# Three score banks in batch 0, fillers accumulating in the value bank, and the small sum instructions on one engine

## The chip, the cores and the metric

One NeuronCore of one Trainium2 chip runs the whole program. TensorE (PE in the profile) multiplies and writes to PSUM, a small memory of eight banks. ScalarE (ACT), VectorE (DVE) and GpSimd (POOL) do the element-wise work, the first two also out of PSUM; SyncE (SP) issues the loads and stores. The metric is the device time of one execution in microseconds; a profile shows one such execution.

## What is computed

The reference is an attention over a window of 128 keys, a gated block with a convolution over three positions, and a second gated block with a causal convolution over five positions. Shapes: 4 batches, 8 heads of 64, 576 positions, model width 512, inner width 1024.

```python
scores = scale * np.matmul(q, k.transpose(0, 1, 3, 2))
scores = np.where(mask, scores + bias[None], -1000000000.0)
attn = np.exp(scores - np.max(scores, axis=-1, keepdims=True))
attn = attn / (np.sum(attn, axis=-1, keepdims=True) + 1e-09)
x = np.matmul(attn, v)                      # heads joined to width 512

h = np.maximum(x @ w_in, 0.0)               # first block
conv = sum(conv_w[k] * shifted(h, k - 1) for k in range(3))
x = (h * sigmoid(conv)) @ w_out

pre = sum(conv_w2[k] * shifted(x, k - 4) for k in range(5))
out = (sigmoid(pre) * (x @ w_val)) @ w_out2 # second block
```

The weights come in double precision, and the kernel works to about single precision: each operand of a large product is split into a high and a low part, and three products (high by high, high by low, low by high) are added in PSUM.

## The kernel before

The work is cut into eight units: four batches (`b`), each in two parts of the sequence (`u` = 0: positions 0 to 255, `u` = 1: the rest). Attention for one unit runs over four pairs of heads; the dense part of a unit runs `hidden` (x by `w_in`, relu, convolution, gate), `mixed` (by `w_out`, second convolution), `valued` (by `w_val`) and `output` (by `w_out2`) in this order. While one unit's dense part runs, the next unit's attention is worked in between.

**Attention of one pair** (`attention`, lines 490 to 682). Blocks of 64 queries of both heads are taken two at a time as a group; a group's scores lie in one PSUM bank of the ring `ps_s` (tiles `pss`). L546 multiplies q by k, L550 adds the bias `bm` and finds the row minimum of the negated scores, L558 takes the exponential and its row sum on ScalarE, L561 (on VectorE) or L563 (on GpSimd) adds 1e-9 to the group's sums and scales them (an instruction on 128x2 numbers), and the reciprocal L568 on VectorE follows. In batch 0 (`turn`) the exponentials are transposed on TensorE: L576 (VectorE) or L577 (GpSimd) makes a unit matrix scaled by the reciprocals (`dg`), L584 multiplies by it into the same `pss` bank, and L590 (ScalarE) and L592 (VectorE) read the high and the low part out to `pt`. In the other batches L609 and L611 scale in place and a DMA transposes. L651 multiplies by V into the one bank `psx`, and L667, or L672 and L674, read that bank out as x.

**V's scale** (`vmax`, `vscale`). V is loaded (tile `gts` for the first half of batch 0, `raw` else), L444 takes its maximum on VectorE, L459 and two small matmuls (L464 and L478, which also write to `psx`) bring it to every partition, and L482 or L483 reads it out.

**Weights** (`widen`, lines 374 to 411). A piece of 128x512 weights arrives as double precision in a `raw` buffer (three of them, 512 KB each) and is turned into single precision by two instructions on ScalarE (L390, L392) and two on VectorE (L394, L403), then split by a copy (L409 on ScalarE or L410 on GpSimd) and a subtraction on GpSimd (L368). There are 24 such pieces, 8 of `w_in`, 8 of `w_out`, 4 of `w_val` and 4 of `w_out2`, and they are all worked while batch 0 runs.

**What sets the order.** `Program` (lines 39 to 209) plans all instructions in lists with costs of its own: each step has an engine, or a choice of engines (L565 gives such a choice), a cost, a priority and the keys it reads and writes. The plan gives each engine's queue its order, and every engine works its queue strictly in that order. A ring of buffers hands them out in the order of the program; `spare = (20,)` on `ps_s` (L321) holds the last of the three banks back for the first 20 groups, which are those of batch 0, so that these use two banks.

**Fillers.** Where the plan shows TensorE idle for more than 250 ns, `warm` (lines 855 to 860) puts matmuls on the zero tile `idle` into TensorE's queue. They go to the third `pss` bank, which nobody else uses until batch 1, and they stop at the first score that needs it (`first`, L862).

## Time and profile before

| | us |
|---|---|
| median of three runs | 455.79 |
| lowest and highest of the three | 453.82, 456.14 |
| the profiled execution's own time | 454.31 |
| its span, first to last instruction | 452.5 |
| busy in the span: TensorE | 436.9 |
| VectorE | 342.7 |
| ScalarE | 319.9 |
| GpSimd | 201.9 |

The 1.8 us between the profiled execution's time and its span lie around the instructions. TensorE's busy time contains the fillers (193 of them, 25.9 us by the profile's count, in which neighbours overlap), so it is no measure of useful work in the early part. The profile's views that follow are the busy times by stretch, the instructions in order of time for one engine, the list of waits, and the list for one source line.

### The profile page before, as it was taken

What the parts mean: (1) busy time and instruction counts of PE and PEld (TensorE: products, weight loads), DVE (VectorE), ACT (ScalarE), POOL (GpSimd) and SP (SyncE); (2) the same over time, 40 slices, a digit from 0 to 9 for tenths busy, and PEclk for the clock granted to TensorE, in tenths of its full rate; (3) what the DMA queues carried; (4) which work ended last, traced back from release to release, by engine and by line L of the source; (5) the groups of instructions that cost most, each with busy time, mean ns of one, the idle gap of its engine ahead of it and who ended that gap; (6) DMA issues with size and microseconds to landing.
All of it is one profiled execution on the core that took longest, in us unless ns stands there. A gap on an engine that the chain in (4) does not pass through costs nothing.

```text
span 452.5 us, 10277 instructions
## 1 busy us (share of the span) xinstructions
PE 436.9 (97%) x3605; PEld 412.1 (91%) x3605; DVE 342.7 (76%) x1056; ACT 319.9 (71%) x930; POOL 201.9 (45%) x341
## 2 busy tenths in 40 slices
PE   7988999999999999999999999999999999999997
PEld 5667888899999999999999999998999998998996
DVE  5799988998977558995969479967979487917390
ACT  2799999964867668785974578677956576847442
POOL 1477898881553327030560436041722164454511
PEclk9999999999999999999999999999999999999999
DMA  8665757557264525658441527395352429350001
GB/s 268 221 233 198 236 171 236 178 183 250 81 100 99 129 67 114 163 128 173 132 81 49 110 77 134 103 189 138 63 112 67 128 64 170 90 119 1 0 1 59
DMA packets 75235, 57.85 MB, mean 128 GB/s; under 512 B 55984, under 2 KB 65968, under 8 KB 75184
## 3 DMA queue, kind: packets, MB, share of 16 engines
q1 hardware_dynamic: 75184, 57.21, 48.6%
q8 instruction: 28, 0.46, 0.4%
q14 instruction: 23, 0.19, 0.1%
HBM read 39.10 MB, written 4.72 MB: 97 GB/s over the span
## 4 chain that ended last, share of the span: by engine, by line
PE 59%; DVE 15%; ACT 13%; DMA 7%; issue 4%; POOL 1%; SPq 0%; DVEq 0%; ACTq 0%; POOLq 0%
PE pm L691 17%; PE pm L692 15%; PE pm L693 15%; PE pss L546 5%; DVE gts L353 4%; PE psx L651 4%; DMA pt<-p 3%; DVE t L353 2%; ACT sg L390 2%; DMA raw<-in_w_in 2%; DVE pss L550 1%; ACT pss L558 1%; PE pss L584 1%; ACT pm L392 1%; DMA raw<-in_w_val 1%
## 5 line engine op out<-in xcount | busy, mean ns | idle before, releaser
L691 PE MATMUL pm<-x,win 128*128 128x256 f32 (+1 forms) x256 | 80.9, 316 | 2.1 <-DVE t L353 2.0
L691 PE MATMUL pm<-g,wout 128*128 128x254 f32 (+1 forms) x256 | 79.8, 312 | 0.2
L692 PE MATMUL pm<-g,wout 128*128 128x254 f32 (+1 forms) x256 | 76.1, 297 | 0.0
L692 PE MATMUL pm<-x,win 128*128 128x256 f32 (+1 forms) x256 | 76.0, 297 | 0.0
L693 PE MATMUL pm<-x,win 128*128 128x256 f32 (+1 forms) x256 | 75.8, 296 | 0.0
L693 PE MATMUL pm<-g,wout 128*128 128x254 f32 (+1 forms) x256 | 75.7, 296 | 0.0
L353 DVE SCALAR_TENSOR_TENSOR t<-pm,cc,t 128x325 f32<-128x325 f32 (+3 forms) x112 | 56.1, 513 | 15.1 <-ACT t L346 11.9
L368 POOL TENSOR_TENSOR g<-t,g 128x254 fp32r<-128x254 f32 (+1 forms) x64 | 51.9, 814 | 28.2 <-ACT g L337 25.5
L546 PE MATMUL pss<-qk 128*128 128x192 f32 (+2 forms) x288 | 57.5, 322 | 3.9 <-DVE pt L592 3.0
L550 DVE CUSTOM_DVE_ANT_0 pss<-pss,bm 128x192 f32<-128x192 f32 (+2 forms) x144 | 47.9, 339 | 14.9 <-PE pss L546 12.9
L563 POOL TENSOR_SCALAR st<-st 128x2 f32<-128x2 f32 (+1 forms) x56 | 11.1, 199 | 103.6 <-ACT pss L558 87.8
L353 DVE SCALAR_TENSOR_TENSOR gts<-pm,cc,gts 128x322 f32<-128x322 f32 (+4 forms) x120 | 57.2, 506 | 0.1
L558 ACT ACTIVATE pss<-pss,st 128x192 f32<-128x192 f32 (+2 forms) x108 | 40.7, 377 | 17.2 <-DVE st L550 15.8
L691 PEld LDWEIGHTS pm<-x,win 128*128 128x128 f32 x256 | 48.2, 188 | 5.0 <-DVE t L353 3.4
L546 PEld LDWEIGHTS pss<-qk 128*128 128x128 f32 x288 | 44.3, 192 | 7.4 <-DVE pt L592 5.7
L691 PEld LDWEIGHTS pm<-g,wout 128*128 128x128 f32 x256 | 48.2, 188 | 1.6 <-ACT pm L392 0.3
L692 PEld LDWEIGHTS pm<-g,wout 128*128 128x128 f32 x256 | 48.5, 190 | 0.0
L693 PEld LDWEIGHTS pm<-g,wout 128*128 128x128 f32 x256 | 48.5, 190 | 0.0
L692 PEld LDWEIGHTS pm<-x,win 128*128 128x128 f32 x256 | 48.3, 189 | 0.0
L693 PEld LDWEIGHTS pm<-x,win 128*128 128x128 f32 x256 | 48.2, 188 | 0.0
L611 DVE SCALAR_TENSOR_TENSOR p<-pss,st,p 128x192 f16<-128x192 f32 (+1 forms) x103 | 36.4, 386 | 12.8 <-DMA pt<-p 9.0
L609 ACT ACTIVATE p<-pss,st 128x192 f16<-128x192 f32 (+1 forms) x103 | 35.9, 403 | 14.0 <-DMA pt<-p 10.2
(109 smaller groups left out, 1172.4 us busy)
## 6 DMA issues: line engine op xcount, KB each, us to landing
qk<-in_qk SPq DMA_DIRECT2D x16, 544.0 KB, 3.7
qk<-in_qk SPq DMA_DIRECT2D x16, 384.0 KB, 3.5
raw<-in_w_out SPq DMA_DIRECT2D x12, 512.0 KB, 4.0
vr<-in_vN SPq DMA_DIRECT2D x16, 256.0 KB, 3.0
raw<-in_w_in SPq DMA_DIRECT2D x8, 512.0 KB, 3.9
raw<-in_vN SPq DMA_DIRECT2D x8, 384.0 KB, 4.4
out<-t SPq DMA_DIRECT2D x16, 161.0 KB, 1.9
raw<-in_w_val SPq DMA_DIRECT2D x4, 512.0 KB, 3.5
```

The source lines that it names most:

```text
L353: pg.add("DVE", dve_t(n, 0 if isinstance(scalar, float) else 1), lambda: nc.vector.scalar_tensor_tensor(out=out, in0=in0, scalar=scalar, i ...
L368: "POOL": (pool_t(n, True), lambda: nc.gpsimd.tensor_tensor(out=lo, in0=src, in1=hi.bitcast(F32), op=ALU.subtract))}
L546: return [nc.tensor.matmul(out=o, lhsT=q_t[:, i, :], rhs=k_t[:, kc:kc + nkey], start=True, stop=True, skip_group_check=True) for i, o, nke ...
L550: pg.add("DVE", 128 + 1.05 * nkey, lambda i=i, s=s, nkey=nkey: nc.vector.tensor_tensor_reduce(out=s, in0=s, in1=bm[:, p, 192 - nkey:192], ...
L558: pg.add("ACT", act_t(nkey, True, 2), lambda i=i, s=s, to=to: nc.scalar.activation(out=to, in_=s, func=AF.Exp, scale=-1.0, bias=stt[:, 0, ...
L563: "POOL": (165, lambda a=a, e=e: nc.gpsimd.tensor_scalar(stt[:, 2, a:e], stt[:, 1, a:e], 1e-9, 1.0 / PSC, op0=ALU.add, op1=ALU.mult))}
L609: pg.add("ACT", act_t(nkey, True, 1), lambda i=i, s=s, hi=hi: nc.scalar.activation(out=hi, in_=s, func=AF.Copy, scale=stt[:, 2, i:i + 1]), ...
L611: pg.add("DVE", dve_t(nkey, 1), lambda i=i, s=s, hi=hi, lo=lo: nc.vector.scalar_tensor_tensor(out=lo, in0=s, scalar=stt[:, 2, i:i + 1], in ...
L651: r.append(nc.tensor.matmul(out=oap, lhsT=lhs, rhs=rhs, start=(i == first[h]), stop=(i == last[h]), skip_group_check=True))
L691: return [nc.tensor.matmul(out=o, lhsT=wh, rhs=hi, start=first, stop=False), nc.tensor.matmul(out=o, lhsT=wh, rhs=lo, start=False, stop=Fa ...
L692: nc.tensor.matmul(out=o, lhsT=wh, rhs=lo, start=False, stop=False),
L693: nc.tensor.matmul(out=o, lhsT=wl, rhs=hi, start=False, stop=last)]
```

## The change

Five edits that belong together. The third bank is no longer held back, so that batch 0's scores use three banks. The fillers move to columns 320 to 511 of the bank `psx`, and only the first of them starts an accumulation; the others add zeros. They read 96 columns of `idle` twice (192 columns and not 256), and the tile shrinks to 128 columns. They are put into every planned pause up to a fixed point of the plan (`FILL`), and no longer up to the first use of the third bank. And the small instruction on the sums has only GpSimd to run on.

```diff
--- before.py
+++ after.py
@@ -24,6 +24,7 @@
 KG = 2
 RAWS = 3
 TURN = 1
+FILL = 80000.0
 RW = 2 * WC
 
 
@@ -291,7 +292,7 @@
     eye = st("eye", [128, 128], F32)
     one = st("one", [NP, 128], F32)
     bm = st("bm", [128, NP, 192], BF16)
-    idle = st("idle", [128, 256], BF16)
+    idle = st("idle", [128, 128], BF16)
 
     GMAX, XMAX = 326, 328
     ring_raw = Ring("raw", RAWS, [128, 2 * WC], U32)
@@ -318,7 +319,6 @@
     ps_m = Ring("pm", 7 - 3, [128, 512], F32, ps)
     ps_m.spare = (16, 16)
     ps_s = Ring("pss", 3, [128, 512], F32, ps)
-    ps_s.spare = (20,)
     ring_pw = Ring("pm", 0, None, None)
     ring_pw.t = ps_m.t[2:4]
     ps_x = Ring("psx", 1, [128, 512], F32, ps)
@@ -562,7 +562,7 @@
                        stt[:, 2, a:e], stt[:, 1, a:e], 1e-9, 1.0 / PSC, op0=ALU.add, op1=ALU.mult)),
                    "POOL": (165, lambda a=a, e=e: nc.gpsimd.tensor_scalar(
                        stt[:, 2, a:e], stt[:, 1, a:e], 1e-9, 1.0 / PSC, op0=ALU.add, op1=ALU.mult))}
-            use = ('DVE', 'POOL')
+            use = ('POOL',)
             pg.add(use, tuple(how[x][0] for x in use), tuple(how[x][1] for x in use),
                    pr, tuple((stk, 1, i) for i in g), ((stk, 2, gi),), port=True)
             pg.add("DVE", 100, lambda a=a, e=e: nc.vector.reciprocal(stt[:, 2, a:e], stt[:, 2, a:e]),
@@ -852,21 +852,25 @@
                 prepare(b2, base - 10000)
             attentions(b2, u2, base + (9588.0 if (b, u) == (0, 0) else 0.0), t - base)
     order = pg.order()
+    filled = []
+
     def warm(t, end):
 
+
+
         while t + 250.0 < end:
-            nc.tensor.matmul(out=ps_s.t[-1][:, 0:256], lhsT=idle[:, 0:128], rhs=idle, start=True, stop=True,
+            nc.tensor.matmul(out=ps_x.t[0][:, 320:512], lhsT=idle[:, 0:128], rhs=bass.AP(idle.tensor, idle.offset, [list(idle.ap[0]), [0, 2], [1, 96]]), start=not filled, stop=True,
                              skip_group_check=True)
+            filled.append(1)
             t += 125.0 if t > 940.0 + 3600.0 else 220.0
 
-    first = next((o.start for o in order if o.eng == "PE" and any(k[0] == ps_s.name + "2" for k in o.wkeys)), 0.0)
     pe = None
     with tc.manual_schedule():
         for o in order:
             if o.eng == "PE":
                 if pe is None:
                     pe = 940.0
-                if o.start < first:
+                if o.start < FILL:
                     warm(pe, o.start)
                 pe = o.start + o.dur
             o.fn()
```

Since the plan is made anew, the queues change in many places. In the built programs the fillers go from 193 to 116, and five of the new ones wait for VectorE or ScalarE, which read the bank `psx`; 80 small instructions on the sums stand on GpSimd where 56 did, and VectorE has none where it had 24. Up to the first matmul with `w_val`, TensorE's queue holds the same dense matmuls; it holds 42 score blocks in place of 35 (five more of 192 columns, one of 128, one of 64), 64 products with `dg` in place of 54, and 168 value matmuls in place of 128. Up to the fourth `mixed` copy of the first unit (L752), ScalarE's queue holds seven exponentials more (five of 192), three copies L590 more (one 256 wide, two 512), two 256-wide and three 512-wide copies of V and one scaling L667 more; fewer are two copies each of x and of g, one pair L390 and L392, two copies L409 of weights, one tanh L761 and one L483. Up to the same point VectorE treats eight score blocks more. Up to the first subtraction L368 of `valued`, GpSimd's queue holds 21 instructions L563 and held 11. On SP, V's first load goes from the fifth place to the second, ahead of `bm`, and the third piece of `w_in` goes ahead of the fourth load of q and k.

At the start of VectorE's queue, a piece from before (`pss0`, `pss1` and `pss2` are the three score banks, `st0` and `st1` the sums, `vmx` the maxima of V, `dg0` to `dg2` the scaled unit matrices; ISA is the bias with its minimum):

```order
L568 RECIPROCAL st0_113<-st0_113 128x2
L550 ISA pss1_126,st0_113<-pss1_126,bm_72 128x192
L550 ISA st0_113 128x1
L576 TENSOR_SCALAR dg1_117<-eye_70,st0_113 128x128
L444 TENSOR_REDUCE vmx_109<-gts_104 128x4
L568 RECIPROCAL st0_113<-st0_113 128x2
L592 TENSOR_TENSOR pt0_119<-pss0_125,pt0_119 128x2x128
L576 TENSOR_SCALAR dg0_116<-eye_70,st0_113 128x128
L444 TENSOR_REDUCE vmx_109<-raw1_75 128x2
```

The queue now begins, right behind its memsets:

```order
L795 MEMSET idle_73 128x64
L444 TENSOR_REDUCE vmx_109<-gts_104 128x4
L550 ISA pss0_125,st0_113<-pss0_125,bm_72 128x64
L550 ISA st0_113 128x1
L550 ISA pss0_125,st0_113<-pss0_125,bm_72 128x128
L550 ISA st0_113 128x1
```

The maximum of V's first load stood behind the first group's scores and stands now ahead of the first score.

On ScalarE, the way to the third piece of `w_in` (`raw0` in the last row) from the second pair's exponentials, before (L517 scales V; `raw1` and `raw2` hold the first two pieces):

```order
L558 ACTIVATE p0_115,st1_114<-pss1_126,st1_114 128x192 x2
L390 ACTIVATE sg1_78<-raw1_75 128x512
L392 ACTIVATE pm3_124<-raw1_75 128x512
L558 ACTIVATE p0_115,st0_113<-pss0_125,st0_113 128x64
L558 ACTIVATE p0_115,st0_113<-pss0_125,st0_113 128x128
L390 ACTIVATE sg0_77<-raw2_76 128x512
L392 ACTIVATE pm2_123<-raw2_76 128x512
L590 ACTIVATE pt1_120<-pss1_126 128x512
L517 ACTIVATE gts_104<-gts_104,vsc_110 128x256
L390 ACTIVATE sg1_78<-raw0_74 128x512
```

The same stretch now:

```order
L558 ACTIVATE p0_115,st1_114<-pss0_125,st1_114 128x192 x2
L390 ACTIVATE sg1_78<-raw1_75 128x512
L392 ACTIVATE pm3_124<-raw1_75 128x512
L558 ACTIVATE p0_115,st0_113<-pss1_126,st0_113 128x64
L558 ACTIVATE p0_115,st0_113<-pss1_126,st0_113 128x128
L390 ACTIVATE sg0_77<-raw2_76 128x512
L392 ACTIVATE pm2_123<-raw2_76 128x512
L590 ACTIVATE pt1_120<-pss0_125 128x512
L667 ACTIVATE t0_95<-psx0_128,vsc_110 128x256
L558 ACTIVATE p0_115,st0_113<-pss2_127,st0_113 128x192 x2
L590 ACTIVATE pt0_119<-pss1_126 128x2x128
L390 ACTIVATE sg1_78<-raw0_74 128x512
```

The scaled output of the first pair (L667), two exponentials from the third bank and a copy to `pt0` came ahead of that piece.

On GpSimd, the end of the subtractions for `w_in` before (`win0` and `win1` are the high and the low part):

```order
L368 TENSOR_TENSOR win1_62<-gts_104,win0_61 128x512
L577 TENSOR_SCALAR dg2_118<-eye_70,st0_113 128x128
L368 TENSOR_TENSOR win1_62<-gts_104,win0_61 128x512
L410 TENSOR_SCALAR win0_61<-gts_104 128x512
L368 TENSOR_TENSOR win1_62<-gts_104,win0_61 128x512
L410 TENSOR_SCALAR wout0_63<-gts_104 128x512
L563 TENSOR_SCALAR st0_113<-st0_113 128x2
L368 TENSOR_TENSOR wout1_64<-gts_104,wout0_63 128x512
L577 TENSOR_SCALAR dg0_116<-eye_70,st0_113 128x128
L577 TENSOR_SCALAR dg1_117<-eye_70,st0_113 128x128
```

About the same place now:

```order
L368 TENSOR_TENSOR win1_62<-gts_104,win0_61 128x512
L410 TENSOR_SCALAR win0_61<-gts_104 128x512
L368 TENSOR_TENSOR win1_62<-gts_104,win0_61 128x512
L563 TENSOR_SCALAR st0_113<-st0_113 128x2
L410 TENSOR_SCALAR win0_61<-gts_104 128x512
L577 TENSOR_SCALAR dg1_117<-eye_70,st0_113 128x128
L563 TENSOR_SCALAR st0_113<-st0_113 128x2
L368 TENSOR_TENSOR win1_62<-gts_104,win0_61 128x512
L577 TENSOR_SCALAR dg1_117<-eye_70,st0_113 128x128
L563 TENSOR_SCALAR st0_113<-st0_113 128x1
```

Of the small instructions L563 there was one between the subtractions, and now there are two, and a third right behind.

## Rows read from the trace of the kernel before

**Rows 1.** Busy time by stretch, whole core.
```profile
core 0: us, PE busy (x) PEld busy (x) DVE busy (x) ACT busy (x) POOL busy (x), PEclk, DMA share, GB/s
0.00:5.00 5.00, 2.87 (x14) 2.25 (x15) 1.11 (x3) 1.28 (x1) 0.83 (x8) 1.00 0.58 157
5.00:22.00 17.00, 15.55 (x119) 12.26 (x119) 13.44 (x49) 9.36 (x34) 6.03 (x16) 1.00 0.79 268
22.00:91.50 69.50, 64.04 (x569) 55.62 (x567) 63.55 (x173) 67.08 (x168) 59.33 (x83) 1.00 0.64 210
91.50:440.00 348.50, 345.24 (x2852) 333.12 (x2847) 263.57 (x830) 239.09 (x723) 132.64 (x232) 1.00 0.46 107
```
**Rows 2.** SP's issues in order of time: start, length, instruction.
```profile
1.19 0.42 SPq L796 DMA_DIRECT2D bm<-in_bias  x1
...
2.60 0.66 SPq L443 DMA_DIRECT2D gts<-in_vN  x1
```
**Rows 3.** VectorE in order of time, with the idle time before and its releaser.
```profile
5.56 0.23 DVE L550 CUSTOM_DVE_ANT_0 pss<-pss,bm 128x64 f32<-128x64 f32 x1 [3.48 <-PE pss L546]
...
8.35 1.22 DVE L444 TENSOR_REDUCE vmx<-gts 128x4 f32<-128x1024 f32 x1 [0.30 <-DMA gts<-in_vN]
```
**Rows 4.** ScalarE in order of time, 18 to 26 us.
```profile
18.55 0.78 ACT L390 ACTIVATE sg<-raw 128x512 f16<-128x512 f32 x1
19.19 0.65 ACT L392 ACTIVATE pm<-raw 128x512 f32<-128x512 f32 x1
19.77 0.58 ACT L590 ACTIVATE pt<-pss 128x512 f16<-128x512 f32 x1
...
21.95 0.78 ACT L390 ACTIVATE sg<-raw 128x512 f16<-128x512 f32 x1 [1.20 <-DMA raw<-in_w_in]
...
23.39 0.62 ACT L409 ACTIVATE win<-gts 128x512 fp32r<-128x512 f32 x1
23.91 0.46 ACT L667 ACTIVATE t<-psx,vsc 128x256 f32<-128x256 f32 x1
24.27 0.50 ACT L517 ACTIVATE gts<-gts,vsc 128x256 f32<-128x256 f32 x1
24.67 0.41 ACT L337 ACTIVATE x<-t 128x256 fp32r<-128x256 f32 x1
25.08 0.42 ACT L558 ACTIVATE p<-pss,st 128x192 f32<-128x192 f32 x1
...
25.49 0.41 ACT L558 ACTIVATE p<-pss,st 128x192 f32<-128x192 f32 x1
```
**Rows 5.** TensorE in order of time, from two stretches.
```profile
11.69 1.69 PE L858 MATMUL pss<-idle 128*128 128x256 bf16 x14
...
77.84 0.61 PE L584 MATMUL pss<-dg,p 128*128 128x128 f32 x4
78.29 0.82 PE L546 MATMUL pss<-qk 128*128 128x192 f32 x4
78.94 0.61 PE L584 MATMUL pss<-dg,p 128*128 128x128 f32 x4
79.48 1.04 PE L651 MATMUL psx<-pt,v 128*64 128x128 f16 x30
80.45 0.94 PE L858 MATMUL pss<-idle 128*128 128x256 bf16 x7
```
**Rows 6.** Line L561 (first), then waits from 0 to 95 us.
```profile
L561 DVE TENSOR_SCALAR st<-st x24: 140/170/860, 16.7 to 397.8; 128x2 f32<-128x2 f32 x18, 128x1 f32<-128x1 f32 x6
...
PEld pss L546 <- DVE pt L592: 5.7, 10, 1.6
...
DVE st L568 <- POOL st L563: 1.1, 3, 0.7
```
**Rows 7.** GpSimd and VectorE in order of time, around 59 us.
```profile
58.77 1.27 POOL L368 TENSOR_TENSOR wout<-gts,wout 128x512 fp32r<-128x512 f32 x1
...
59.21 0.86 DVE L561 TENSOR_SCALAR st<-st 128x2 f32<-128x2 f32 x1
```

## The prediction

> **What bounds the kernel now.** I read the profile in the order in which it narrows things down: first the busy time of each engine by stretch, then who waits for whom at the start, then single instructions for their prices. The stretches [rows 1] show two regimes. From 91.5 us to 440 us TensorE is busy for 345.2 of 348.5 us: there the kernel is bound by TensorE, and nothing else matters unless it makes TensorE wait. Before that it is not. From 22 to 91.5 us ScalarE is busy 67.1 of 69.5 us, VectorE 63.6, GpSimd 59.3: the weights are being widened on these three engines while batch 0's softmax and the first unit's element-wise work share them. TensorE's 64.0 busy us there hold fillers, the matmuls on the zero tile `idle` that write nothing anybody reads (14 of them take 1.69 us at 11.69, 7 take about 0.9 us at 80.45 [rows 5]). And before 22 us ScalarE is busy only 9.4 of 17 us: it waits for the first scores and for loads, and its last wait there, 1.20 us, is for the third piece of `w_in` [rows 4].
>
> So the time is: the moment at which TensorE becomes the bound (91.5 us, the first matmul with `w_val`), plus TensorE work that is then left. Two things shorten it: ScalarE getting to that moment with less idle time, and more of TensorE's work being done by then. Fillers taken away by themselves give nothing, since TensorE was not the bound where they stood.
>
> **The change, part by part.** *Fewer and shorter fillers.* 193 become 116, of 192 columns in place of 256. None stands behind the place of the first `w_val` matmul in either order. I cost this at nothing. The cover is the element-wise work above; if a filler gives way to waiting, TensorE waits instead.
>
> *The fillers' new place.* They now write to the bank `psx`, which the value matmuls and the two small matmuls of the value scale use. In the order five of them wait for VectorE or ScalarE to have read that bank; before, only the first waited for anything (its operand). Behind a waiting filler stand scores and the matmuls that turn the exponentials round. The readers they wait for are early in their own queues, so I take 0; the upper bound is five times the longest wait of TensorE's scores for VectorE to be done with a bank, 1.6 us [rows 6], 8.0 us in all. All five stand where ScalarE and not TensorE is the bound, and two of them where even ScalarE has idle time; that is the cover.
>
> *The third bank.* This is what moves the work. By the first `w_val` matmul the new order has the same dense matmuls behind it, and more attention: seven more score blocks (five of 192 columns, one of 128, one of 64), ten more 128-column products with the scaled unit matrices, and 40 more value matmuls. Prices, start to start [rows 5]: two 192-column blocks (the profile has two records for each such matmul) take 0.65 us (78.29 to 78.94), so 0.33 each and 0.22 and 0.11 for the smaller ones, 2.0 us; two unit-matrix products take 0.45 us, so ten take 2.2 us; 30 value matmuls take 0.97 us (79.48 to 80.45), so 40 take 1.3 us. Sum: 5.5 us of TensorE work that no longer lies in the stretch that TensorE bounds.
>
> That has a price on ScalarE, whose queue ahead of the fourth copy of the first unit's `mixed` (the last thing that `w_val` needs of it) grows. More: seven exponentials with their sums at 0.41 us (25.08 to 25.49 [rows 4]; the two narrow ones a little less), 2.6; three copies out of the turned bank, 0.58 us long of which 0.1 overlaps the next, one of them half as wide, 1.2; three 512-wide and two 256-wide copies of V at 0.52 and 0.41, 2.4; one scaled output at 0.36. Fewer: two copies of x and two of g at 0.41, 1.6; one widening pair at 0.64 and 0.58, 1.2; two copies of weights at 0.52, 1.0; one tanh, about 0.4; a small copy, 0.1. Net +2.3 to +2.5 us; I take 2.5.
>
> *The start.* Ahead of the third `w_in` piece ScalarE now does two more exponentials, one more copy out of the turned bank, one more scaling and one more copy of V and one more scaled output: 0.8 + 0.3 + 0.4 + 0.4 + 0.4, less a 0.1 us copy that goes to VectorE, 2.2 us. If that piece starts at 21.95 as now, these 2.2 us fill idle time. Against it: the order puts batch 0's V load second on SP's queue, ahead of `bm`, and the reduction of V ahead of every score on VectorE. Today V is issued at 2.60 [rows 2] and its reduction starts when it has landed, at 8.35, 5.75 us later; the first score is treated at 5.56 [rows 3]. If V takes the same 5.75 us from an issue at 1.19, where `bm` is issued now, and the reduction its 1.22 us, the first score is treated at 8.2, 2.6 us later, with the exponentials, the turned products and every bank behind it. It can land sooner, as only one load is ahead of it, not four. ScalarE has 7.6 us of idle time before 22 us to take the delay up, and the third `w_in` piece now stands ahead of the fourth q and k load on SP's queue, not behind it, so that its 1.20 us wait may shrink. So this term lies between +2.2 us (all filled) and -0.4 us (all the delay comes through); I take +1.0, between them, because both effects act on the same idle stretch.
>
> *The small instructions.* 24 additions and scalings on the sums (128x2) leave VectorE, seven of them before 110 us; VectorE took 0.14 to 0.86 us for one, 0.17 in the median [rows 6]. Why up to 0.86 is in one pair of rows [rows 7]: at 59.21 such an instruction runs to 60.07, and GpSimd's 1.27 us subtraction, begun at 58.77, ends at 60.04. [...] VectorE's own queue ahead of the same point grows by eight score treatments and three low halves, and loses one widening pair; its 5.9 us of idle time [rows 1] cover that, so the relief buys slack and no time. On GpSimd 21 of these stand ahead of the first subtraction of `valued` and not 11: ten times 0.19 us is 1.9 us, against 10.2 us idle. Cost: nothing, as long as the reciprocal that waits for it on VectorE is not late. That wait is 1.1 us in three times before 95 us now [rows 6].
>
> **Sum.** 5.5 - 2.5 + 1.0 = 4.0 us less. The profiled execution took 454.31 us (452.5 us of span); the median of the three runs is 455.79, and it is the median that I carry the difference to: 455.8 - 4.0 = 451.8 us. With the ends of the start's term it is 450.6 to 453.2. Behind 91.5 us the new order also shuffles the work; TensorE stands idle 3.3 us between 91.5 and 440 us now, so that stretch can give back about 3 us at most, and I allow the same for a loss.
>
> **Rivals.** *It stays where it is.* The early delay comes through (-0.4) and the extra attention meets late inputs, so that only half of the 5.5 us is done by then: 2.7 - 2.5 - 0.4 gives -0.2, 456.0 us. For it: ScalarE at 97% has no room, and a queue that is in order stops at the first late row. Against it: ScalarE still waited 2.4 us there, and the third bank takes away what made TensorE wait most there: scores waiting for a bank whose low half VectorE had yet to read, 5.7 us in ten times [rows 6].
>
> *Slower: the reciprocals stand behind GpSimd.* GpSimd's queue is in order, and 1.27 us subtractions of weights stand between these small instructions [rows 7]. If each of the ten added ones is met by one, VectorE stands still ten times 1.27, 12.7 us, of which its 5.9 us of idle time cover a part; 6.8 us come through, and with the 4.0 us gain that is 455.8 + 2.8 = 458.6 us. It decides from about eight such meetings. For it: in the piece of GpSimd's order shown above one of them stands directly behind such a subtraction. Against it: the three waits that exist average 0.4 us.
>
> [...]
>
> That the change does not do what it says I leave out: the order has scores of batch 0 in all three banks.
>
> **Chances.** Forecast (with its ends and the late shuffle, 447.5 to 453.5): 0.60. It stays: 0.24. Slower by GpSimd's queue: 0.13. The clock: 0.03. A measurement of this kernel can tell about 0.5%, 2.3 us, from no change. The range from 447.5 to 457.5 takes in the forecast with the 3 us of the shuffle downward and the case in which nothing changes. Faster 0.61, same 0.24, slower 0.15.
>
> **What would show it.** Right: the first `w_val` matmul starts near 91 us as now, with 5 us more attention done; ScalarE busier than 9.4 us between 5 and 22 us; VectorE's reciprocals wait for GpSimd about as often as now. Wrong: the first score treated after 8 us and the third `w_in` piece on ScalarE after 23 us (the start's term); the first `w_val` matmul after 95 us (the trade of 5.5 against 2.5); reciprocals waiting for GpSimd by over 5 us before 95 us (the slower rival); a granted clock under 1.00 anywhere; over 6 us of idle TensorE between there and 440 us (the shuffle).

## The result and the profile after

The changed kernel takes 447.5 us (median of four runs, 447.11 to 448.72), 0.984 of the kernel before (95% interval 0.980 to 0.988), which took 454.95 us beside it (median of four). Taken once more beside the later experiments it takes 447.06 us, 0.9815 (0.979 to 0.984). The prediction was 451.8 us, range 447.5 to 457.5. The sign and the trade behind the first `w_val` held. The gain, 7.5 us, is nearly twice the 4.0 us of the sum, and the median lies on the very end of the range.

The profiled execution took 447.63 us with a span of 445.6 us, 6.9 us less than before. The busy times by stretch of the changed kernel (columns as in [rows 1]):

```profile
5.00:22.00 17.00, 13.96 (x112) 11.48 (x111) 13.34 (x51) 11.12 (x41) 7.37 (x20) 1.00 0.85 279
22.00:91.50 69.50, 62.43 (x583) 56.12 (x583) 64.65 (x187) 67.28 (x176) 62.31 (x99) 1.00 0.66 212
91.50:440.00 348.50, 346.01 (x2812) 335.58 (x2812) 254.54 (x790) 239.36 (x711) 137.38 (x244) 0.99 0.48 106
...
90.00:95.00 5.00, 3.56 (x21) 3.38 (x22) 4.65 (x13) 4.83 (x13) 3.77 (x5) 0.69 0.61 216
95.00:100.00 5.00, 5.00 (x28) 4.95 (x28) 3.17 (x6) 2.54 (x7) 4.10 (x5) 0.63 0.39 98
100.00:105.00 5.00, 5.00 (x43) 4.90 (x41) 4.78 (x20) 3.13 (x14) 2.20 (x5) 1.00 0.97 337
```

ScalarE (fourth busy time) works 11.12 us between 5 and 22 us where it worked 9.36 [rows 1]. And the granted clock, 1.00 in every stretch before, is 0.69 and 0.63 between 90 and 100 us. TensorE in order of time there:

```profile
88.07 0.47 PE L651 MATMUL psx<-pt,v 128*64 128x128 f16 x10
90.19 0.35 PE L691 MATMUL pm<-g,wval 128*128 128x254 f32 x1 [1.65 <-ACT t L363]
90.38 0.29 PE L692 MATMUL pm<-g,wval 128*128 128x254 f32 x1
90.50 0.28 PE L693 MATMUL pm<-g,wval 128*128 128x254 f32 x1
...
93.10 0.58 PE L691 MATMUL pm<-g,wval 128*128 128x254 f32 x1 [1.24 <-DVE gts L776]
93.47 0.42 PE L692 MATMUL pm<-g,wval 128*128 128x254 f32 x1
93.69 0.41 PE L693 MATMUL pm<-g,wval 128*128 128x254 f32 x1
...
98.38 0.80 PE L546 MATMUL pss<-qk 128*128 128x192 f32 x3
```

The first `w_val` matmul starts at 90.19 (before: 91.53), behind a pause of 1.65 us; after a second pause of 1.24 us the matmuls stand 0.21 us apart and not 0.12, at a granted clock of 0.50 (from 93.10 to 98.38 us). Up to 98.38 that are 24 of them, 24 x (0.21 - 0.12) = 2.2 us lost in this execution. It is not in all of them: two of the four show a mean granted clock of 1.000 (447.11 and 447.36 us) and two 0.992 (447.63, the one shown, and 448.72), so that in the times the fall is worth about 1 us.

In the kernel before, the same place was reached in another way. TensorE, and then VectorE and ScalarE:

```profile
89.99 0.92 PE L546 MATMUL pss<-qk 128*128 128x192 f32 x4 [0.51 <-DVE pt L592]
90.84 0.76 PE L651 MATMUL psx<-pt,v 128*64 128x128 f16 x20
91.53 0.39 PE L691 MATMUL pm<-g,wval 128*128 128x254 f32 x1
...
89.86 0.47 DVE L353 SCALAR_TENSOR_TENSOR gts<-pm,cc,gts 128x250 f32<-128x250 f32 x1
...
90.09 0.39 ACT L752 ACTIVATE g<-pm 128x254 fp32r<-128x254 f32 x1
```

The same two of the changed kernel:

```profile
89.58 0.47 DVE L353 SCALAR_TENSOR_TENSOR gts<-pm,cc,gts 128x250 f32<-128x250 f32 x1
...
89.99 0.38 ACT L752 ACTIVATE g<-pm 128x254 fp32r<-128x254 f32 x1
```

In both built programs the first `w_val` matmul writes to the PSUM bank that held the third `mixed` product, and it waits until VectorE has read that bank for the last time (L353, a step of the second convolution). The fourth copy L752 is needed only by the tenth `w_val` matmul. The trace agrees: in the changed kernel the first `w_val` starts at 90.19, 0.14 us after the end of L353 (89.58 + 0.47 = 90.05) and before the copy ends (90.37). So the wait that the row of 90.19 puts down to ScalarE's L363 is one for VectorE. In the kernel before, L353 ended at 90.33 and `w_val` came only 1.20 us later: it stood behind a score block that waited for one of the two banks, and behind 20 value matmuls.

**Where the 6.9 us are.** First `w_val` 1.34 us earlier (91.53 to 90.19): 0.28 because VectorE's L353 ends earlier, and 1.06 because TensorE's own queue no longer stands in front of it. From there to the end of the span it is 355.4 us in place of 361.0, 5.6 less. Rows of that part, of the changed kernel and of the kernel before:

```profile
90.19:445.60 355.41, 349.25 (x2832) 338.56 (x2832) 255.64 (x792) 241.44 (x717) 138.69 (x246) 0.99 0.48 107
```

```profile
91.53:452.50 360.97, 354.36 (x2912) 342.01 (x2906) 264.52 (x832) 242.16 (x729) 135.74 (x235) 1.00 0.45 105
```

TensorE has 80 matmul records fewer in it (2832 and 2912), is busy for 5.1 us less, although the clock costs it 2.2 us here, and is idle for 0.5 us less. That makes 7.3 us less work at a granted clock of 1.00, of which the 5.5 us of attention that is done ahead explain the larger part; the other 1.8 us were not followed up.

### The profile page after: what moved, and what is told of

The parts are those of the page before. It is cut to its first block, busy times and chain, and to the rows that moved or that the text cites. A ratio compares the mean times of both kernels' runs of the same rounds, so it can differ in the third digit from the quotient of the medians.

```text
span 445.6 us, 10132 instructions
## 1 busy us (share of the span) xinstructions
PE 427.3 (96%) x3528; PEld 407.4 (91%) x3528; DVE 333.6 (75%) x1029; ACT 319.9 (72%) x929; POOL 207.9 (47%) x369
## 4 chain that ended last, share of the span: by engine, by line
PE 66%; DVE 12%; ACT 11%; DMA 5%; POOL 3%; issue 2%; SPq 0%; DVEq 0%; ACTq 0%; POOLq 0%
PE pm L691 20%; PE pm L692 18%; PE pm L693 18%; PE pss L546 6%; PE psx L651 3%; DMA pt<-p 2%; DVE t L353 2%; DVE pss L550 2%; ACT p L558 2%; DVE gts L353 2%; ACT sg L390 2%; ACT pm L392 1%; DMA gts<-in_vN 1%; DMA raw<-in_w_val 1%; DVE gts L403 1%
## 5 line engine op out<-in xcount | busy, mean ns | idle before, releaser
L353 DVE SCALAR_TENSOR_TENSOR t<-pm,cc,t 128x253 f32<-128x253 f32 (+3 forms) x112 | 56.1, 513 | 19.1 <-ACT t L346 15.9
L368 POOL TENSOR_TENSOR g<-t,g 128x254 fp32r<-128x254 f32 (+1 forms) x64 | 51.8, 812 | 22.7 <-ACT g L337 20.1
L353 DVE SCALAR_TENSOR_TENSOR gts<-pm,cc,gts 128x322 f32<-128x322 f32 (+4 forms) x120 | 58.3, 510 | 2.7 <-ACT g L752 2.4
L339 POOL TENSOR_SCALAR g<-t 128x254 fp32r<-128x254 f32 (+1 forms) x38 | 16.7, 438 | 64.7 <-DVE t L353 46.3
L563 POOL TENSOR_SCALAR st<-st 128x2 f32<-128x2 f32 (+1 forms) x80 | 15.8, 198 | 65.5 <-ACT pss L558 57.8
```

What stands on the lines that cost most here:

```text
L339: "POOL": (pool_t(n), lambda: nc.gpsimd.tensor_scalar(hi, src, 1.0, 0.0, op0=ALU.mult, op1=ALU.add))}
L353: pg.add("DVE", dve_t(n, 0 if isinstance(scalar, float) else 1), lambda: nc.vector.scalar_tensor_tensor(out=out, in0=in0, scalar=scalar, i ...
L368: "POOL": (pool_t(n, True), lambda: nc.gpsimd.tensor_tensor(out=lo, in0=src, in1=hi.bitcast(F32), op=ALU.subtract))}
L563: "POOL": (165, lambda a=a, e=e: nc.gpsimd.tensor_scalar(stt[:, 2, a:e], stt[:, 1, a:e], 1e-9, 1.0 / PSC, op0=ALU.add, op1=ALU.mult))}
```

## The experiments

The kernel before took 454.97, 455.62 and 455.27 us (medians) in the three series in which the kernels ran; each experiment is put beside the one of its series. The repeated run of the changed kernel belongs to the third series, with the narrower fillers and the two plans made anew; a variant of the other two series is compared with the changed kernel by the ratios, and the two ratios of the changed kernel, 0.984 and 0.9815, then give two differences. The first `w_val` matmul, what follows it in the span (both from the one profiled execution) and the attention that its order has ahead of `w_val` (in the prediction's prices, 26.0 us for the order before) stand in one table. The profiled execution can lie off the median, by 1.8 us upward without fillers and 1.1 us downward with the small instructions on VectorE:

| kernel | median, us | ratio to before (95%) | first `w_val` | from there | attention ahead |
|---|---|---|---|---|---|
| before | 455.3 | | 91.5 | 361.0 | 26.0 |
| narrower fillers only | 454.9 | 0.999 (0.998 to 1.001) | 91.5 | 361.2 | 26.0 |
| filler edits only | 457.6 | 1.006 (1.004 to 1.008) | 94.1 | 361.6 | 26.0 |
| the same, three banks, old order | 457.4 | 1.004 (1.003 to 1.006) | 94.1 | 361.8 | 26.0 |
| before, planned anew | 456.0 | 1.002 (1.000 to 1.004) | 91.4 | 364.0 | 26.0 |
| GpSimd edit only | 453.3 | 0.996 (0.994 to 0.998) | 92.5 | 359.0 | 27.9 |
| changed, planned anew | 451.9 | 0.993 (0.990 to 0.995) | 91.5 | 358.2 | 29.6 |
| changed, without the GpSimd edit | 450.1 | 0.989 (0.985 to 0.993) | 91.6 | 357.7 | 31.5 |
| changed, small instructions on VectorE | 450.0 | 0.989 (0.986 to 0.992) | 92.0 | 355.1 | 31.5 |
| changed, no fillers | 451.2 | 0.991 (0.989 to 0.993) | 91.7 | 359.4 | 31.5 |
| changed, more fillers | 449.1 | 0.987 (0.984 to 0.990) | 91.5 | 355.0 | 31.5 |
| changed, V's reduction later | 448.1 | 0.985 (0.982 to 0.987) | 91.0 | 354.6 | 31.5 |
| changed, again | 447.1 | 0.982 (0.979 to 0.984) | 89.6 | 355.3 | 31.5 |

**Theory and rivals.** The theory is the prediction's: the third bank lets the plan do more attention ahead of `w_val`, and the rest is worth nothing. The rivals: the small instructions make the gain; the fillers do; the waits for a bank themselves were the price, whatever the order; the new plan was a lucky draw.

### Without the last edit

```diff
-            use = ('POOL',)
+            use = ('DVE', 'POOL')
```

> The changed kernel with its last edit undone: the small instructions on the sums may go to VectorE or GpSimd as before; three banks and the new fillers stay. Theory (the third bank, and the order that is planned with it, makes the gain): 447 to 450 us, the first w_val matmul near 90 to 92 us with about 5 us more attention done by then. Rival one (moving the small instructions off VectorE makes the gain): 453 to 456 us. Rival two (each re-made plan is a draw, and this one was lucky): anywhere from 446 to 456 us, with no more attention done by w_val.

450.1 us, 0.1 above what the theory gave: three banks and the new fillers alone bring 4.9 us, with the 5.5 us of attention ahead of `w_val`. The last edit brings another 2.3 or 3.4 us by the ratios, where the prediction had nothing; the interval of this run meets that of the first series of the changed kernel (up to 0.988) and not that of the second. The executions of this run also differ in the granted clock, and the time goes with it, from 447.5 us at a mean of 1.000 to 453.4 at 0.985. So a part of the 2.3 to 3.4 us is clock, and how large a part was not separated.

### The last edit alone

```diff
-            use = ('DVE', 'POOL')
+            use = ('POOL',)
```

> The kernel before with one edit alone: the small instructions on the sums run on GpSimd only; two banks and the old fillers stay. Theory: no gain that can be told, 453 to 457 us. Rival one (the small instructions make the gain): 447 to 450 us. Rival two (the draw of the plan): anywhere from 448 to 460 us. In its order batch 0's first V load stands seventh on SP and not fifth, so a part of any difference can come from there.

453.3 us, at the lower edge of the theory's range, but 1.7 less than before and outside no change by its interval. Its plan is another one too and has 1.9 us more attention ahead of `w_val`, so this run doesn't tell which of the two brought it.

### The engine of the small instructions, with the order held

```diff
-                   "POOL": (165, lambda a=a, e=e: nc.gpsimd.tensor_scalar(
+                   "POOL": (165, lambda a=a, e=e: nc.vector.tensor_scalar(
```

> The changed kernel's plan kept as it is, but each of the 80 small instructions on the sums is issued on VectorE at the same place of the plan. Theory (the engine of these instructions is slack on both): 447 to 449 us, within 0.3% of the changed kernel, TensorE's start of w_val within 0.7 us of its 90.2. Rival (VectorE is relieved, or meets GpSimd less): 3 us or more slower than the changed kernel, 450.5 us and up.

450.0 us, 2.2 or 3.3 us more than the changed kernel by the ratios (the interval meets the first of its two and not the second): nearly the rival's 3 us, and the theory's "slack on both" falls. It is not the clock alone: the one execution with a mean granted clock of 1.000 took 448.2 us, the three of the changed kernel 446.3 to 447.4. The busy times of this kernel from 22 to 91.5 us:

```profile
22.00:91.50 69.50, 60.53 (x566) 54.39 (x565) 67.28 (x197) 65.39 (x172) 57.37 (x81) 1.00 0.61 203
```

VectorE (third busy time) is at 67.28 of 69.5 us, 64.65 in the changed kernel. The small instructions alone, on VectorE in that stretch (busy time and count):

```profile
22.00:91.50 69.50, 5.57 (x16) 1.00 0.61 203
```

The 16 take 5.57 us, 0.35 each, twice the median of 0.17 that the prediction gives. (The 24 of the kernel before took 7.76 us, 0.32 each: the mean was there to be read.) Two rows, of VectorE and of GpSimd, show the longest of them:

```profile
24.03 1.22 DVE L563 TENSOR_SCALAR st<-st 128x2 f32<-128x2 f32 x1
...
23.96 1.26 POOL L368 TENSOR_TENSOR win<-gts,win 128x512 fp32r<-128x512 f32 x1
```

A 128x2 instruction on VectorE that starts 0.07 us after a GpSimd subtraction lasts until 25.25; the subtraction ends at 25.22. It is the picture of [rows 7] again. Of the 16, twelve are 128x2; six of these take 0.36 us or more, and each of the six ends within 0.03 us of the end of a GpSimd instruction. The four of 128x1 take 0.13 to 0.14 us, three of them while a GpSimd instruction runs. The rows show which instructions end together; what holds the 128x2 form back was not shown.

One of the six stands directly ahead of the L353 for which the first `w_val` waits, and that is how the delay gets through:

```profile
91.04 0.41 DVE L563 TENSOR_SCALAR st<-st 128x2 f32<-128x2 f32 x1
91.37 0.47 DVE L353 SCALAR_TENSOR_TENSOR gts<-pm,cc,gts 128x250 f32<-128x250 f32 x1
```

L353 ends at 91.84 and `w_val` starts at 91.98. A VectorE without slack is also late for ScalarE, whose waits between 22 and 92 us are now:

```profile
ACT sg L390 <- DMA raw<-in_w_in: 0.9, 1, 0.9
...
ACT p L558 <- DVE st L550: 0.7, 1, 0.7
ACT sg L390 <- DMA raw<-in_w_val: 0.6, 1, 0.6
```

In the program VectorE's widening is the last reader of a `raw` buffer, so a late VectorE can also let the next load of weights start late: the two waits for loads shown are 0.9 and 0.6 us, 0.3 and 0.4 us in the changed kernel. ScalarE's idle time in the stretch goes from 2.2 to 4.1 us, and the first `w_val` from 89.6 or 90.2 to 92.0.

### The fillers of the change in the kernel before

```diff
-            nc.tensor.matmul(out=ps_s.t[-1][:, 0:256], lhsT=idle[:, 0:128], rhs=idle, start=True, stop=True,
+            nc.tensor.matmul(out=ps_x.t[0][:, 320:512], lhsT=idle[:, 0:128], rhs=bass.AP(idle.tensor, idle.offset, [list(idle.ap[0]), [0, 2], [1, 96]]), start=not filled, stop=True,
...
```

(The run also has the smaller `idle` tile and the fixed point `FILL`; the 193 fillers stay.)

> The kernel before with the filler edits alone: the same number of fillers at the same places of the same order, but 192 columns wide, accumulating in the value bank; two banks for the scores, small instructions as before. Theory (the place and width of the fillers cost and bring nothing, as ScalarE is the bound where they stand): 454 to 456 us, within 0.3% of before. Rival (fillers that wait for the value bank's readers, or that hold TensorE up, matter): over 1.5 us away from before on either side, up to the 8 us bound of the prediction.

457.6 us, 2.6 more: the rival, on the slow side. The waits of its TensorE up to 92 us hold what the prediction had bounded by 8.0 us and then taken as 0 (the lines are those of this kernel, one more than before):

```profile
PE psx L863 <- DVE x L675: 1.5, 2, 1.3
...
PE psx L863 <- ACT t L668: 1.3, 1, 1.3
...
PE psx L863 <- ACT x L673: 0.5, 1, 0.5
```

Together 3.3 us in which TensorE's queue stands at a filler, with scores behind it. In the profiled execution the clock also falls, to 0.72 and 0.50 in the stretches from 24 to 28 us; that is not the cause, as the four executions with a mean granted clock of 1.000 took 456.4 to 457.7 us.

### Their width alone

```diff
-            nc.tensor.matmul(out=ps_s.t[-1][:, 0:256], lhsT=idle[:, 0:128], rhs=idle, start=True, stop=True,
+            nc.tensor.matmul(out=ps_s.t[-1][:, 0:192], lhsT=idle[:, 0:128], rhs=idle[:, 0:192], start=True, stop=True,
```

> The kernel before with fillers of 192 columns and not 256, in their old bank, where nobody waits for them or makes them wait; the order is row for row the old one. It parts the two filler edits, which together cost 2.6 us. Theory (fillers in the value bank wait for its readers, and that is the cost): 454 to 456 us, granted clock 1.00 in 22 to 37 us. Rival (the shorter fillers leave longer pauses and the clock falls): 456.5 to 458.5 us, with a granted clock near 0.5 somewhere between 22 and 37 us.

454.9 us, granted clock 1.00 between 22 and 37 us, first `w_val` at 91.5: the width costs nothing. What is left for the 2.6 us is the new bank with the accumulation in it and the operand that is read twice. The 3.3 us of waits make the bank the likely one; the rest was not tried by itself.

### Three banks under the old order

```diff
             gp, sk = ps_s.next()
+            if ps_s.i <= 15:
+                gp = ps_s.t[(ps_s.i - 1) % 3]
```

> The kernel before with the filler edits and with three score banks under the old order: the plan is made with two banks, every queue keeps its order row for row, but the first 15 groups of batch 0 take the three banks in turn. It stands against the run with the filler edits alone (457.6 us). Theory (the bank is worth something only through the order it lets the plan make, with more attention ahead of w_val): 456 to 458.5 us, first w_val at 93 to 95 us, as in that run. Rival (the waits of scores for a bank are themselves the price, 5.7 us in ten times in the kernel before): 452 to 455 us, first w_val at 89 to 92 us.

457.4 us beside 457.6 (ratios 1.004 and 1.006), first `w_val` at 94.1 in both: the theory's number. The waits of scores for a bank (5.7 us in the kernel before, [rows 6]) are gone from its trace up to 92 us, and nothing is gained. TensorE waits elsewhere instead, in the list of waits and at one place in order of time:

```profile
PE psx L865 <- ACT t L670: 3.6, 2, 1.8
PE psx L865 <- DVE x L677: 2.5, 2, 1.3
...
29.75 2.14 PE L865 MATMUL psx<-idle 128*128 128x192 bf16 x13 [1.83 <-ACT t L670]
31.68 1.54 PE L549 MATMUL pss<-qk 128*128 128x192 f32 x4
```

With two shorter ones (0.6 and 0.4 us) the fillers wait 7.1 us here and 3.3 in the run with the filler edits alone, 3.8 us more. So the run does not part theory and rival: what the scores no longer wait for, the fillers behind them wait for, and these fillers may hide a gain that the three banks would have with fillers that nobody holds up. The program's eight banks (`pm` four, `pss` three, `psx` one) are all in use, so that wasn't tried.

### No fillers

```diff
-FILL = 80000.0
+FILL = 0.0
```

> The changed kernel without any filler. Theory (the fillers only hold TensorE's clock at its upper level in the pauses): the granted clock falls below 1.00 in several of the stretches 5 to 22, 22 to 91.5 us, and the time is 449 to 454 us, a few us that come through where TensorE's chain of scores and turned products is late. Rival one (fillers cost as much as they give, since those in the value bank wait): 445 to 448 us. Rival two (the clock stays down through the whole early part and TensorE becomes the bound): 465 us and up.

451.2 us, 3.2 or 4.4 us more than with them by the ratios (its interval meets neither of the changed kernel's): theory. The clock falls, to 0.69 between 30 and 35 us, behind a stretch in which TensorE is busy for 2.61 of 5 us:

```profile
25.00:30.00 5.00, 2.61 (x24) 2.16 (x24) 4.12 (x13) 4.72 (x14) 4.68 (x8) 0.97 0.77 255
30.00:35.00 5.00, 5.00 (x30) 4.79 (x27) 4.84 (x13) 3.83 (x11) 4.00 (x8) 0.69 0.67 211
```

In the repeated run of the changed kernel both stretches have 1.00. The profiled execution is the slowest of the six (453.0 us), and its span is 6.2 us longer than that of the repeated run: 2.2 ahead of `w_val` (91.7 and 89.6) and 4.1 behind it (359.4 and 355.3), where its clock falls again, to 0.70 from 95 to 100 us and to 0.98 from 400 to 440 (1.00 in the repeated run). How much of the median's loss is clock and how much lateness was not separated.

### More fillers, to hold the clock at `w_val`

```diff
-FILL = 80000.0
+FILL = 100000.0
```

> The changed kernel with fillers up to 100000 in place of 80000 of the plan's time: 27 more, of which 11 stand directly ahead of the first w_val matmul and 16 behind it in the next two pauses; all else is row for row the same. Theory (the fall of the clock to 0.63 to 0.69 between 90 and 100 us costs about 2 us): granted clock 1.00 there and 444.5 to 447 us. Rival (the fillers stand in the way of w_val by as much, or TensorE is waiting for VectorE and ScalarE there anyway): 447 to 449 us.

449.1 us, 1.3 or 2.4 us more than the changed kernel by the ratios, with intervals that meet: no gain, and so the rival. TensorE's queue shows why:

```profile
87.64 0.47 PE L651 MATMUL psx<-pt,v 128*64 128x128 f16 x10
90.63 1.18 PE L862 MATMUL psx<-idle 128*128 128x192 bf16 x11 [2.52 <-ACT x L672]
91.52 0.56 PE L691 MATMUL pm<-g,wval 128*128 128x254 f32 x1
91.88 0.42 PE L692 MATMUL pm<-g,wval 128*128 128x254 f32 x1
```

The fillers that were to bridge the pause stand behind ten value matmuls in the same bank and wait 2.52 us for ScalarE to read it out. So the pause stays, the clock falls all the same (0.66 from 90 to 95 us), and then 11 fillers run, 0.9 us from the first to `w_val`. By VectorE's L353, which ends at 89.51 here, `w_val` could have started at about 89.7 and starts at 91.52.

### The start: V's reduction behind the first scores

```diff
...
+    order.remove(v_max)
+    order.insert(order.index(dve[3]) + 1, v_max)
...
```

(`v_max` is the reduction L444 of the tile `gts`, `dve` the list of VectorE's instructions on PSUM banks; what depends on it follows.)

> The changed kernel with one instruction moved: the reduction of batch 0's first V on VectorE stands behind the first four score blocks and not ahead of them; the loads and all else keep their order, but for what depends on it. Theory (that reduction holds the first scores back from about 5.6 to 8.3 us, and ScalarE's start with them): first score treated before 6.5 us, first w_val 0.5 to 1.5 us earlier than 90.2, 445.5 to 447 us. Rival (the delay is absorbed: the turned products wait for GpSimd, whose scaling of V's maxima stands ahead of the first small instruction, or ScalarE then waits for the third w_in piece): first w_val within 0.4 us of 90.2 and 447 to 448.5 us.

448.1 us, 0.4 or 1.5 us more than the changed kernel by the ratios, with intervals that meet: no gain, as the rival had it, though the first `w_val`, 91.0, is not within its 0.4 us of 90.2. The scores are treated sooner, at 6.78 where the changed kernel has 8.29, now held by the load of `bm`. But ScalarE, which starts 1.5 us earlier (7.50, not 9.00), loses it again at once:

```profile
7.50 0.31 ACT L560 ACTIVATE p<-pss,st 128x64 f32<-128x64 f32 x1 [5.48 <-DVE st L552]
...
11.97 0.31 ACT L560 ACTIVATE p<-pss,st 128x64 f32<-128x64 f32 x1 [2.78 <-PE pss L586]
...
14.15 0.60 ACT L592 ACTIVATE pt<-pss 128x512 f16<-128x512 f32 x1 [0.50 <-PE pss L586]
...
16.53 0.38 ACT L592 ACTIVATE pt<-pss 128x256 f16<-128x256 f32 x1 [0.69 <-PE pss L586]
```

It waits for the turned products, 4.0 us in all where the changed kernel has 1.68 (below). Of the 1.5 us gained at the start 1.1 are lost in the first of these waits. The last two fall where TensorE was slow in this execution: its granted clock is 0.90 from 5 to 22 us (1.00 in the changed kernel), and four records of 192-column scores take 1.54 us from 14.22 on, 0.92 from 17.60 on. They may come from that. The two executions of this run with a mean clock of 0.999 and 1.000 took 447.6 and 447.0 us, as the changed kernel does: the delay of the first scores was absorbed in a later wait anyway.

### Both kernels planned anew

```diff
-            pg.add("DVE", 100, lambda a=a, e=e: nc.vector.reciprocal(stt[:, 2, a:e], stt[:, 2, a:e]),
+            pg.add("DVE", 105, lambda a=a, e=e: nc.vector.reciprocal(stt[:, 2, a:e], stt[:, 2, a:e]),
```

The kernel before with this line:

> The kernel before with its plan made anew through a change that does nothing by itself: the planner counts the reciprocal as 105 ns and not 100. All five queues come out in another order, with the same 35 score blocks, 54 turned products and 128 value matmuls ahead of the first w_val matmul. Theory (what counts is how much attention is done ahead of w_val, and a re-made plan alone is worth little): 453.5 to 457 us. Rival (each plan is a draw of several us, and the changed kernel drew well): below 452 or above 459 us.

The changed kernel with it:

> The changed kernel with its plan made anew in the same way (reciprocal counted as 105 ns): 38 score blocks, 64 turned products and 138 value matmuls ahead of the first w_val matmul, 29.6 us of attention by the prediction's prices where the changed kernel has 31.5 and the kernel before 26.0. Theory (the three banks bring it, through the attention done ahead): 448 to 451.5 us. Rival (the changed kernel drew well): 453 us and up.

456.0 and 451.9 us. The first is within 0.2% of the kernel before. The second is 4.9 us slower than the changed kernel, a little outside what the theory gave, and faster than every two-bank plan by 1.4 us or more, though its interval (0.990 to 0.995) meets that of the two-bank plan with the GpSimd edit (0.994 to 0.998). In the table, what a plan takes follows the attention that it has ahead of `w_val`: 455.3 less the surplus over 26.0 gives 453.4 for 27.9 (measured 453.3), 451.7 for 29.6 (451.9) and 449.8 for 31.5 (450.1 and 450.0). That is a series of plans, not an experiment with that quantity alone. The changed kernel lies 2.7 us below that line. Two plans on the line, those of 453.3 and 451.9, have all small instructions on GpSimd as the changed kernel has, so that edit is not worth 2.7 us in every plan. For this part of the gain the rival stands: with the same five edits and a plan made anew, 3.4 us of 455.3 are gained and not 8.2.

### The changed kernel again

> The changed kernel once more, unaltered, beside the others on the same chip, so that differences of 2 us between its variants can be read. 447 to 449 us by every theory; if it stands at 449 to 450, the runs with the small instructions on VectorE (450.0), with more fillers (449.1) and with the moved reduction (448.1) differ from it by less than can be told.

447.06 us, with 446.34 and 447.21 as ends; it stays the fastest of all, by the median.

## Why the prediction was right, and where it was too small

**The bound and the trade** held. Time was "the moment of the first `w_val` matmul plus what TensorE has left", in all kernels of the table: the first `w_val` lies between 89.6 and 94.1, and what the kernels gain or lose beside that they gain or lose behind it. The rest is 5.6 us shorter, and the 5.5 us of attention are the larger part of the 7.3 us of work that left it; that the two first numbers are so near is luck, as the clock took 2.2 us back. That the order and not the waits for a bank brings it is argued from these counts. The old order with three banks does not settle it, as its fillers took up what the scores no longer waited for.

**The size** is in part luck. The low end of the range, on which the median lies, was there for 3 us of shuffle, and that gave 0.8 (below). What filled it were the terms that follow and the plan: the same edits in a plan made anew gain 3.4 us, near the 4.0 us of the sum.

**The first `w_val`** was put by the sum at 91.5 + 2.5 - 1.0 = 93.0 (the prediction's list of signs says "near 91 us", which does not fit that sum) and came at 90.2, 2.8 us earlier. Three terms, with ScalarE's fourth `mixed` copy as the mark that the prediction chose:

- *The start*, taken as +1.0 between +2.2 and -0.4, was +2.1, near the upper end. Up to the last `mixed` copy ScalarE is idle 11.72 us (89.99 less busy times of 12.40 and 65.87) where it was idle 13.78 (90.09 less 10.64 and 65.67). The first score is treated at 8.29, forecast 8.2, and the third `w_in` piece is reached at 21.88, as before [rows 4], with the extra work done. VectorE and ScalarE of the changed kernel:

```profile
7.16 1.22 DVE L444 TENSOR_REDUCE vmx<-gts 128x4 f32<-128x1024 f32 x1 [5.15 <-DMA gts<-in_vN]
8.29 0.22 DVE L550 CUSTOM_DVE_ANT_0 pss<-pss,bm 128x64 f32<-128x64 f32 x1
...
9.00 0.31 ACT L558 ACTIVATE p<-pss,st 128x64 f32<-128x64 f32 x1 [6.99 <-DVE st L550]
12.37 0.31 ACT L558 ACTIVATE p<-pss,st 128x64 f32<-128x64 f32 x1 [1.68 <-PE pss L584]
...
21.88 0.82 ACT L390 ACTIVATE sg<-raw 128x512 f16<-128x512 f32 x1
```

  ScalarE's one long wait is at the very start; from 13 us on it hardly stops. The prediction added a delay of 2.6 us to a chain that had its waits behind that point, and should have asked which later wait the delay would use up.
- *ScalarE's longer queue*, -2.5, was -2.0 (78.27 busy to that copy, 76.31 before).
- *Not in the sum*: `w_val` stands 0.20 us behind the start of the copy where it stood 1.44 us behind it. The prediction took that copy for the last thing that `w_val` needs, and the first `w_val` needs it in neither kernel. In the kernel before, TensorE's own queue ended last, at a score that waited for a bank; in the changed kernel it is VectorE's L353.

2.1 - 1.0 + 0.5 + 1.2 = 2.8.

**The small instructions** were costed at nothing, and this is the step that failed: "the relief buys slack and no time". In the changed kernel's order, with all else held, it is worth 2.2 to 3.3 us that VectorE does not run them. The median of 0.17 us hid a mean of 0.32 in the kernel before, and 0.35 next to busy GpSimd in the changed order. VectorE's 5.9 us of idle time in 69.5 were no cover, because the first `w_val` waits for VectorE: with 2.2 us left it reads the bank out later and delays ScalarE too. The reciprocals that wait for GpSimd, the rival's ground, wait less than before:

```profile
DVE st L568 <- POOL st L563: 0.7, 1, 0.7
```

**The fillers' new place**, taken as 0 with a bound of 8.0, costs 2.6 us in the old order, with waits of 0.5 to 1.3 us. In the changed kernel three such waits of 1 us or more stand before 92 us (1.2, 1.0 and 1.0 us); what they cost there was not parted from what the fillers give, 3.2 to 4.4 us in sum.

**The clock** fell, to 0.50 from 93.10 to 98.38 us, which cost 2.2 us in the execution shown and about 1 us between executions with and without it. The prediction gave the clock a chance of 0.03; its list of signs counted any clock under 1.00 as wrong, and by that sign it came out wrong. No filler stands at that place in either order; what is new are the two pauses of 1.65 and 1.24 us, because `w_val` now waits for VectorE and not behind attention of its own. In the repeated run waits of 1.5 and 1.2 us stand there, with a clock of 0.83 from 90 to 100 us; in the run with V's reduction moved they are 1.5 and 1.3 us, and the clock is 1.00. So pauses of that length alone do not decide it, and what does was not shown.

**The shuffle behind** gave back 0.8 of the 3 us allowed: TensorE is idle for 2.5 us between 91.5 and 440 us (348.50 less 346.01) where it was 3.3.

## What to carry to other kernels

Count the work that a new order moves to the other side of the place where the bound changes hands; here that count gave the larger part of the gain, and the disappearance of a wait under the old order, with other waits behind it, gave nothing. Before a change in a starved stretch is given a price, look for the later wait that takes up its delay. At the place where the bound changes hands, read in the program what the first instruction waits for: here it was VectorE, busy for 63.6 of 69.5 us beside a ScalarE at 67.1, and its idle time was no slack. Price an instruction by its mean next to the engine that it meets (0.35 us here), not by its median (0.17). And a filler that writes where other engines read can wait in the very pauses that it was to fill; here such fillers waited 3.3 us, in a run 2.6 us slower.

## What was not expected of the hardware

An instruction on 128x2 numbers took VectorE 0.15 to 1.22 us beside a busy GpSimd (57.4 of 69.5 us), and the six long ones of twelve ended with a GpSimd instruction, to within 0.03 us; on 128x1 it took 0.13 to 0.14 us. On GpSimd, in the changed kernel, the same instructions took 0.19 us in the median and 0.51 at most. TensorE's granted clock was 0.50 (0.21 us from matmul to matmul, not 0.12) behind two pauses of 1.65 and 1.24 us that had 1.7 us of dense matmuls between them, and 1.00 again from 100 us on, after some 5 us of dense work at 0.50. With the same queue, three of the eight executions of the changed kernel show a mean granted clock of 1.000, and so no such fall.
